# Copy of yn laid out by quarters, norm in place, rstd transfers ahead of reloads

## The chip, the cores and the metric

The kernel runs on one core of a Trainium2 chip. The time is device microseconds of one execution. Three runs of the kernel before gave 1457.63, 1461.26 and 1462.50 us; the median is 1461.26 us. The engines are named as in the profile: PE (TensorE), ACT (ScalarE), DVE (VectorE), POOL (GpSimd) and SP (SyncE, which here only issues DMAs; its queue is written SPq).

## The reference

One ConvNeXt V2 block on an image of 512 x 512 pixels with 96 channels, in bf16:

```
out = depthwise 3x3 convolution of x with dw          (96 channels)
h   = (out - mean) / sqrt(var + 1e-5)                 (over the 96 channels of a pixel)
h   = gelu(h @ w1)                                    (96 -> 384)
gx  = sqrt(sum of h*h over all pixels + 1e-6)         (one value for each of 384 channels)
nx  = gx / (mean of gx + 1e-6)
h   = (gamma * (h * nx) + beta + h) @ w2              (384 -> 96)
result = x + h
```

gx needs every pixel before the second matmul can begin, so there are two passes over the image.

## The kernel before, in words

**Units of work.** The image is cut into 128 blocks of four rows; two blocks, eight rows, make a pair d, of which there are 64. The first pass (about 0 to 880 us) goes in slots s: two slots to a pair, one block's matmul and gelu in each. The second pass (about 940 us to the end) takes the 128 blocks again, multiplies by w2 and writes the output.

**First pass, pair d.** SP loads x (`load_x`, four DMAs of 32 partitions into a tile `xin`). DVE turns it so that channels lie on partitions (`turn_x`), PE does the convolution (`conv_taps`), ACT and DVE evacuate it into a tile `y_bf` of [128, 2, 3, 512]. Partition 32q + p holds quarter q (two image rows and 16 channels); the second index, `ee`, is the even or odd channels; the third the group of 32 channels. For odd channels the quarters are turned round by two. POOL squares `y_bf` into `ysq` (`stage_sq`), PE sums both over channels (`stage_stats`), and for each two pairs (a batch k) DVE forms the variance, POOL the reciprocal root (`stage_rstd`, `stage_newton`), and DVE turns it (`stage_turn`).

**rstd and the normalised copy.** `stage_rows` writes the turned rstd to DRAM (`r_dram`, four DMAs for a batch), `stage_bcast` reads it back onto all partitions (`rbc`, four DMAs). `stage_norm` multiplies on POOL `y_bf` by `rbc` into a tile `yn`, once for even and once for odd channels. `stage_write` copies `yn` to DRAM (`yn_dram`): one DMA of 128 partitions for the even channels and two of 64 for the odd ones, whose halves are swapped. `stage_read` (`read_yn`) loads a block back as `ynT`, channels on 96 partitions, in two DMAs. The mean is not subtracted here; the weights `w1p` take it out. The channels of `ynT` come in the order of the planes, and w1 is loaded in that same order by six small DMAs. Six `ynT` tiles go round; 6 `y_bf`, 3 `yn`.

**MLP of the first pass.** `mlp_units` makes of a block six units: PE multiplies `ynT` by `w1p` into PSUM, ACT does the gelu of 128x1024 into `g`. DVE (`bst`) and PE (the gram matrix) gather the sums of squares. One block in three has its `g` stored to DRAM (`g_dram`, three DMAs, `store_next`).

**Order.** The order on each engine is that of the program. What goes into slot s is set by a table (`put`). For the batch of pairs d0 and d0+1 in the steady state: rows in slot 2*d0+7, broadcast in 2*d0+8, norms in 2*d0+9 and 2*d0+11, the writes in the slot after each norm, reloads of the even block one slot after the write and of the odd block two after, its MLP two slots after the reload. So in an odd slot SP issues: four loads of x, a store of `g`, the two reloads of an even block, and then, every second time, four rows. In an even slot: two reloads of an odd block, every second time four broadcasts, the write of the even channels, a store of `g`, the two writes of the odd channels. SP is one queue: an instruction that waits holds up all behind it. At most eight of its DMAs are under way, because they go round eight semaphores and each waits for the one eight places before it.

**Second pass.** Of the 128 blocks one in three has `g` loaded back (`gl`, POOL's queue), five are held, and the others load `ynT` again through `read_yn` (`load_rest`) and recompute `g` into `gr`. POOL adds the bias to x (`xb`), DVE adds it to the product (`o_sb`), SP writes the output.

Of the kernel before, what the change touches and what calls it, by code (L numbers as in the profile page):

```python
# [53 lines left out]
def kernel(  # L54
# [13 lines left out]
    bf16 = x.dtype  # L68
    assert bf16 == mybir.dt.bfloat16

    B, H, W, C = x.shape
# [3 lines left out]
    NI = C // 32  # L75
# [3 lines left out]
    ND = NBLK // 2  # L79
# [3 lines left out]
    QW = GR * 128  # L83
    NQ = GR * W // QW
    dram = ctx.enter_context(tc.tile_pool(name="dram", bufs=1, space=bass.MemoryType.DRAM))
    yn_dram = dram.tile([ND, 2 * NI, 4, 32 * W], bf16, name="yn_dram")
    r_dram = dram.tile([len(BATCHES), R8 * BATCH * W], bf16, name="r_dram")

    TAIL0 = NBLK - NTAIL
# [25 lines left out]
    def quad_out(flat_ap):  # L115
        return flat_ap.rearrange("p (g r m) -> p g r m", r=GR, m=MB)

    PLANE = 4 * 32 * W

    def read_yn(eng, t, q):  # L120
        base = yn_dram[q // 2]
        for h in range(2):
            eng.dma_start(out=t[:C, 2 * h:2 * h + 2, :].rearrange("c r w -> c (r w)"),
                          in_=bass.AP(base.tensor, base.offset + (2 * (q % 2) + h) * 32 * W,
                                      [[2 * W, 16], [PLANE, 2 * NI], [1, 2 * W]]))

    consts = ctx.enter_context(tc.tile_pool(name="consts", bufs=1))
    prepool = ctx.enter_context(tc.tile_pool(name="pre", bufs=1))
# [3 lines left out]
    w1_raw = consts.tile([C, E], bf16, name="w1_raw")  # L132
# [45 lines left out]
    with ExitStack() as p1:  # L178
        pe, dve, act, pool, sp = (InOrder(tc, e) for e in (nc.tensor, nc.vector, nc.scalar, nc.gpsimd, nc.sync))
# [22 lines left out]
        pc = p1.enter_context(ExitStack())  # L202
# [8 lines left out]
        def load_x(d):  # L211
            t = xinpool.tile([128, 2, SL, C], bf16, name="xin")
            off = lambda r, k, s: x.offset + ((R8 * d - 1 + 2 * r + k) * W - 1 + s) * C
            if d in (0, ND):
                k = 1 - d // ND
                if d == 0:
                    dve.memset(t[0:32, 0].rearrange("p g c -> p (g c)").bitcast(f32), 0.0)
                    pool.memset(t[0:1, 1, 0, :], 0.0)
                else:
                    pool.memset(t[0:32].rearrange("p k g c -> p (k g c)").bitcast(f32), 0.0)  # L220
                p0, s0, s1 = (16, 0, 1) if d == 0 else (0, SL - 1, SL)
                a, n = (1, SL - 1) if d == 0 else (0, SL - 1)
                sp.dma_start(out=t[0:32, k, a:a + n, :].rearrange("p g c -> p (g c)"),
                             in_=bass.AP(x.tensor, off(0, k, a), [[PXP * C, 32], [1, n * C]]))
                for p0, p1 in ((1, 16), (16, 32)) if d == 0 else ((0, 16), (16, 31)):
                    sp.dma_start(out=t[p0:p1, k, s0, :],
                                 in_=bass.AP(x.tensor, off(0, k, s0) + p0 * PXP * C, [[PXP * C, p1 - p0], [1, C]]))
            if d == 0:
                for r in range(1, 4):
                    load_pair(t, d, r, act if r > 1 else sp)  # L230
            elif d < ND:
                for r in range(4):
                    load_pair(t, d, r)
            xins[d] = t
# [18 lines left out]
        with nc.allow_low_precision("sums of zeros and a one"):  # L253
            dve.tensor_reduce(out=mask18, in_=ident_f[:18, :18].rearrange("p (k t) -> p k t", k=2), axis=AX.X, op=ALU.add)
            for q in range(4):
                dve.tensor_reduce(out=eye16[32 * q:32 * q + 32, :],
                                  in_=ident_f[32 * q:32 * q + 32, 32 * q:32 * q + 32].rearrange("p (c k) -> p c k", k=2),
# [8 lines left out]

        cen = consts.tile([C, 128], bf16, name="cen")
        xtpool = pc.enter_context(tc.tile_pool(name="xt", side="right", bufs=1))
        ypool = pc.enter_context(tc.tile_pool(name="ybf", side="right", bufs=6))
        ysqpool = pc.enter_context(tc.tile_pool(name="ysq", side="right", bufs=3))  # L270
        small = pc.enter_context(tc.tile_pool(name="small", side="right", bufs=2))
        rtpool = pc.enter_context(tc.tile_pool(name="rt", side="right", bufs=2))
        rbcpool = pc.enter_context(tc.tile_pool(name="rbc", side="right", bufs=3))
        ynpool = pc.enter_context(tc.tile_pool(name="yn", side="right", bufs=3))
        XT = [(0, 2), (2, 3), (5, 2)]
        xt_all = xtpool.tile([128, 7, SL * MB * 2], bf16, name="xT")
        assert 7 * SL * MB * 2 >= NQ * NCH * QW
# [20 lines left out]
        def load_rest(n, sq, pq):  # L298
            q = ORDER[n]
            v = grp.setdefault(q, {})  # L300
            if is_held(q):
                v["g"] = gs[q]
            elif is_whole(q):
                v["g"] = late.gl.tile([128, NQ, NCH, QW], bf16, name="gl")
                pq.dma_start(out=v["g"][:].rearrange("p t j w -> p (t j w)"), in_=g_dram[whole.index(q)])
            else:
                ynt = yn_ring[SLOTS[nth_made[q] % NYT]]
                if q not in KEPT:
                    read_yn(sq, ynt, q)
                v["ynt"] = ynt  # L310
# [92 lines left out]
        for i, (ee, G) in enumerate(UNITS):  # L403
            c0 = 32 * G + ee
            dve.tensor_tensor(out=dwx[:, i].rearrange("p (q c k) -> p q c k", q=4, k=2),
                              in0=dw18[:, None, c0:c0 + 31:2, None].to_broadcast([18, 4, 16, 2]),
                              in1=mask18[:, None, None, :].to_broadcast([18, 4, 16, 2]), op=ALU.mult)
            pe.matmul(Ud[:, i, :], lhsT=dwx[:, i], rhs=taps18, start=True, stop=True)
        for i in range(0, 2 * NI, NI):
            dve.tensor_tensor(out=Wq[:, i:i + NI].rearrange("p i d t (c o) -> p (i d t) c o", o=2),  # L410
                              in0=eye16[:, None, :, None].to_broadcast([128, 6 * NI, 16, 2]),
                              in1=Ud[:, i:i + NI].rearrange("p i (n o) -> p (i n) o", o=2)[:, :, None, :].to_broadcast(
                                  [128, 6 * NI, 16, 2]), op=ALU.mult)

        for ee in range(2):
            for G in range(NI):
                pool.dma_start(out=w1_raw[NI * ee + G:C:2 * NI, :], in_=w1[32 * G + ee:32 * G + 32:2, :])
        pool.dma_start(out=w2_sb[:], in_=w2.rearrange("(j p) c -> p j c", p=128))
        with nc.allow_non_contiguous_dma("tiny gamma/beta load"):
            pool.dma_start(out=gam_bf[:], in_=grn_gamma.rearrange("(j p) -> p j", p=128))  # L420
# [35 lines left out]
        ybf, ysq, yns, rbcs, msts, rns, rts = ({} for _ in range(7))  # L456
# [162 lines left out]
        def stage_rows(k):  # L619
            n = BATCHES[k][1]  # L620
            rt = rts.pop(k)
            with nc.allow_non_contiguous_dma("small rows of rstd"):
                for t in range(2 * n):
                    sp.dma_start(
                        out=r_dram[k, :2 * n * 32 * 128].rearrange("(t q a p) -> t a q p", q=32, a=4, p=32)[t],
                        in_=rt[:, 32 * t:32 * t + 32])

        def stage_bcast(k):
            n = BATCHES[k][1]
            rbc = rbcpool.tile([128, 2, BATCH // 2, W], bf16, name="rbc")  # L630
            base = r_dram[k]
            for q in range(4):
                sp.dma_start(out=rbc[32 * q:32 * q + 32].rearrange("p e d w -> p (e d w)"),
                             in_=bass.AP(base.tensor, base.offset + q * 4 * n * W,
                                         [[0, 16], [2 * n * W, 2], [1, 2 * n * W]]))
            rbcs[k] = rbc

        def stage_norm(d, eng=None):
            k = batch_of[d]
            i = d - BATCHES[k][0]  # L640
            y = ybf.pop(d)
            for ee in range(2):
                yn = ynpool.tile([128, NI, W], bf16, name="yn")
                (eng or pool).tensor_tensor(out=yn[:], in0=y[:, ee],
                                            in1=rbcs[k][:, ee, i:i + 1, :].to_broadcast([128, NI, W]), op=ALU.mult)
                yns[d, ee] = yn

        def stage_write(d, ee):
            yn = yns.pop((d, ee))
            base = yn_dram[d]  # L650
            step = 64 if ee else 128
            for p0 in range(0, 128, step):
                sp.dma_start(out=bass.AP(base.tensor, base.offset + ee * NI * PLANE + (p0 + 64 * ee) % 128 * W,
                                         [[W, step], [PLANE, NI], [1, W]]),
                             in_=yn[p0:p0 + step, :, :])

        def stage_read(b):
            t = yn_ring[b % NYT]
            read_yn(sp, t, b)
            ynts[b] = t  # L660
# [186 lines left out]
        with nc.allow_low_precision("sums of zeros and a one"):  # L847
            dve.tensor_reduce(out=rowsel[:, :R8].rearrange("p (q r) -> p q r", r=2),
                              in_=ident_f[:].rearrange("p (q c r) -> p q r c", q=4, r=2), axis=AX.X, op=ALU.add)
        dve.tensor_copy(out=rowsel[:, R8:], in_=rowsel[:, :GR])  # L850
        load_x(3)
        def next_x(s):
            if s % 2 and (s + 7) // 2 <= ND:
                load_x((s + 7) // 2)

        alone = 0
        for s in range(last_slot + 1):
            get = lambda kind: at.get((s, kind), [])
            early = s < FIRST_MLP + 6
            if not early:  # L860
                next_x(s)
            if early or s % 2 == 0:
                for b in get("read"):
                    stage_read(b)
            for k in get("bcast"):
                stage_bcast(k)
            for d in get("write"):
                stage_write(d, 0)
            store_next()
            for d in get("write"):  # L870
                stage_write(d, 1)
            if early:
                next_x(s)
            elif s % 2:
                for b in get("read"):
                    stage_read(b)
            for k in get("rows"):
                stage_rows(k)
            for k in get("newton"):
                stage_rstd(k, pool)  # L880
                stage_newton(k, pool)
# [2 lines left out]
            for d in get("norm"):  # L884
                stage_norm(d)
            mlp = get("mlp")

            def spread_out():
                for k in get("spread"):
                    stage_spread(k)  # L890
                for d in get("norma"):
                    stage_norm(d, dve)
# [114 lines left out]
        r = gi[:].bitcast(f32)  # L1007
        for it in range(3):
# [5 lines left out]
            r = rn_[:]  # L1014
# [75 lines left out]
```

## Time and profile before

| what | value |
| --- | --- |
| median of three runs | 1461.26 us |
| the profiled execution | 1462.48 us, span 1460.6 us |
| granted clock of the profiled execution | 0.986 |
| busy, whole span | PE 91%, ACT 91%, POOL 89%, DVE 74% |
| DMA moved | 430.82 MB, mean 295 GB/s |
| first pass, 300 to 500 us | ACT 192.09 of 200 us, POOL 191.88, PE 187.33, DMA share 0.93 |
| second pass, 940 to 1200 us | PE 245.22 of 260 us, POOL 242.14, ACT 238.40, DMA share 0.99 |
| `yn_dram<-yn` | 64 DMAs of 384 KB and 128 of 192 KB |
| `ynT<-yn_dram` | 420 DMAs of 192 KB: 268 in the first pass and around the turn, 152 in the second |
| `stage_norm` on POOL (`yn<-y_bf,rbc`) | 124 of 3104 ns |

Almost every instruction carries L36, the line of the helper that records the order, so groups are told apart by tile names. A row of the waits says which engine waited, for whom, how long in total, how many times and the longest. In the timeline of SP the second column is the time that the named DMAs took to issue, waits included; SP moves no data itself.

### The profile page before, as it was taken

The numbers are of one execution on the slowest core, as the hardware profiler recorded it, in microseconds if no ns is written. First come the engines' busy times: TensorE is split into PE (matmuls) and PEld (weight loads), VectorE is DVE, ScalarE is ACT, GpSimd is POOL, SyncE is SP. The second block draws the span as 40 slices with busy tenths as digits, with TensorE's granted clock in tenths as the row PEclk, the third lists the DMA queues.
The fourth block names the chain that finished last, engine by engine and source line by source line (L and its number), as shares of the span: only waits on it lengthen the run. The fifth ranks groups of instructions, "written<-read, shape, count | busy, mean of one in ns | idle before, by whom it ended". The sixth has DMA issues, their size and how long they took to land.

```text
span 1460.6 us, 55999 instructions
## 1 busy us (share of the span) xinstructions
PE 1334.5 (91%) x24212; PEld 871.7 (60%) x24212; DVE 1080.6 (74%) x2052; ACT 1333.3 (91%) x1235; POOL 1299.0 (89%) x899
## 2 busy tenths in 40 slices
PE   7879999999999999989999987889999989899998
PEld 3445555555555555555555554567777667666676
DVE  5768988988889898888889878745555545455455
ACT  4879999999999999999999999989999888888897
POOL 3499999999999999999999995489999999899997
PEclk8899999999999999999999999999999999999999
DMA  7779899998899998999899766499999999999997
GB/s 175 212 219 283 275 286 274 277 287 269 271 299 272 277 290 268 281 280 275 261 275 299 228 190 192 162 355 331 344 373 391 393 383 362 378 378 370 395 366 303
DMA packets 194103, 430.82 MB, mean 295 GB/s; under 512 B 39184, under 2 KB 88944, under 8 KB 188992
## 3 DMA queue, kind: packets, MB, share of 16 engines
q1 hardware_dynamic: 178044, 318.50, 69.6%
q0 software_dynamic: 15616, 108.29, 19.9%
q8 instruction: 190, 3.11, 0.9%
q10 hardware_dynamic: 196, 0.45, 0.1%
q14 instruction: 57, 0.47, 0.1%
HBM read 265.70 MB, written 161.45 MB: 292 GB/s over the span
## 4 chain that ended last, share of the span: by engine, by line
PE 42%; DMA 22%; ACT 18%; POOL 7%; DVE 4%; issue 3%; SPq 2%; ACTq 0%; DVEq 0%; POOLq 0%
PE PS L36 42%; ACT g L36 13%; DMA out_dram<-o_sb 11%; DMA ynT<-yn_dram 7%; ACT y_bf L36 4%; POOL xb L339 3%; DMA xin<-in_x_dram 3%; SPq L36 2%; POOL yn L36 2%; DVE bst L36 2%; DVE o_sb L36 1%; POOL ysq L36 1%; DMA rbc<-r_dram 1%; ACT xT L36 1%; ACT ysq L36 0%
## 5 line engine op out<-in xcount | busy, mean ns | idle before, releaser
L36 ACT ACTIVATE g<-PS 128x1024 bf16<-128x1024 f32 (+1 forms) x722 | 705.5, 1055 | 34.3 <-PE PS L36 20.2
L36 DVE BATCH_NORM_STATS2 bst<-g 128x6 f32<-128x512 bf16 x885 | 547.0, 677 | 46.8 <-ACT g L36 46.7
L36 PE MATMUL PS<-ynT,w1p 128*128 128x512 bf16 x1920 | 544.8, 381 | 39.0 <-ACT g L36 23.0
L36 ACT ACTIVATE gr<-PS 128x1536 bf16<-128x1536 f32 x348 | 485.8, 1450 | 47.6 <-PE PS L36 42.3
L36 DVE TENSOR_TENSOR o_sb<-PS,xb 128x384 bf16<-128x384 f32 x512 | 275.7, 557 | 244.8 <-PE PS L36 172.2
L36 POOL TENSOR_TENSOR yn<-y_bf,rbc 128x1536 bf16<-128x1536 bf16 x124 | 382.3, 3104 | 14.2 <-DMA rbc<-r_dram 13.2
L339 POOL TENSOR_TENSOR xb<-xr,B2c 128x1536 f32<-128x1536 bf16 x118 | 368.4, 3132 | 17.2 <-DVE o_sb L36 15.7
L36 POOL TENSOR_TENSOR ysq<-y_bf 128x1536 bf16<-128x1536 bf16 x120 | 327.1, 2747 | 38.1 <-DVE y_bf L36 38.1
L36 PEld LDWEIGHTS <-gr 128*128 128x128 bf16 x4152 | 206.6, 99 | 82.6 <-issue 31.5
L36 PE MATMUL PS<-xT,Wq 32*32 32x511 bf16 (+1 forms) x9216 | 235.9, 396 | 10.7 <-DVE xT L36 3.8
L36 PEld LDWEIGHTS <-w1p 128*128 128x128 bf16 x1920 | 148.4, 98 | 152.6 <-issue 89.2
L36 PE MATMUL PS<-W2s,gr 128*128 128x96 bf16 x4080 | 216.6, 207 | 23.6 <-DVE o_sb L36 23.3
L36 PE MATMUL PS<-w1p,ynT 128*128 128x384 bf16 (+2 forms) x1272 | 192.7, 273 | 27.6 <-ACT g L36 22.2
L36 PEld LDWEIGHTS <-Wq 32*32 32x32 bf16 x9216 | 100.2, 89 | 142.8 <-issue 64.8
L36 PEld LDWEIGHTS <-g 128*128 128x128 bf16 x2626 | 161.9, 98 | 34.2 <-issue 4.2
L36 PE MATMUL PS<-g 128*128 128x128 bf16 (+1 forms) x2386 | 173.2, 222 | 1.8 <-DVE warm L36 1.2
L36 PEld LDWEIGHTS <-ynT 128*128 128x128 bf16 x1272 | 102.0, 97 | 105.2 <-issue 82.6
L36 ACT ACTIVATE y_bf<-PS 128x1024 bf16<-128x1024 f32 (+1 forms) x141 | 137.4, 984 | 25.2 <-PE PS L36 25.2
L36 DVE STREAM_TRANSPOSE xT<-xin 128x576 f32<-128x576 f32 (+1 forms) x195 | 145.0, 771 | 6.2 <-DMA xin<-in_x_dram 4.9
L36 PEld LDWEIGHTS <-gl 128*128 128x128 bf16 x1824 | 89.4, 98 | 32.3 <-issue 9.4
L36 PE MATMUL PS<-W2s,gl 128*128 128x96 bf16 x1824 | 96.5, 206 | 7.7 <-DVE o_sb L36 7.5
L36 DVE CAST y_bf<-PS 128x512 bf16<-128x512 f32 x115 | 78.1, 679 | 5.8 <-PE PS L36 5.1
(108 smaller groups left out, 571.6 us busy)
## 6 DMA issues: line engine op xcount, KB each, us to landing
ynT<-yn_dram SPq DMA_DIRECT2D x420, 192.0 KB
g_dram<-g SPq DMA_DIRECT2D x114, 512.0 KB
gl<-g_dram POOLq DMA_DIRECT2D x38, 1536.0 KB, 11.3
xin<-in_x_dram SPq DMA_DIRECT2D x253, 216.0 KB
out_dram<-o_sb SPq DMA_DIRECT2D x127, 384.0 KB
xr<-in_x_dram POOLq DMA_DIRECT2D x123, 384.0 KB, 7.1
yn_dram<-yn SPq DMA_DIRECT2D x64, 384.0 KB
yn_dram<-yn SPq DMA_DIRECT2D x128, 192.0 KB
```

The costliest lines, as they stand in the source:

```text
L36: r = f(*a, **k)
L339: pq.tensor_tensor(out=xb[:], in0=grp[q]["xr"][:], in1=bias[:, None, :].to_broadcast([128, PXP, C]), op=ALU.add)
```

## The change

The DRAM copy of the normalised rows has its axes in the order quarter, plane instead of plane, quarter. A pair is written by four DMAs of 32 partitions, each of all six planes (192 KB), instead of one of 128 and two of 64 partitions. A block is read by one DMA for the even and one for the odd channels, each of 48 partitions (every second one) and two quarters, instead of one for each two rows on 96 partitions. The channels of `ynT` are then in their natural order, and w1 is loaded by one DMA. `stage_norm` writes its product over `y_bf`; the tile `yn` is gone, and `y_bf` has seven buffers instead of six. In the slot, broadcasts come before the reload of the odd block, and rows before the reload of the even block.

```diff
-    yn_dram = dram.tile([ND, 2 * NI, 4, 32 * W], bf16, name="yn_dram")
+    yn_dram = dram.tile([ND, 4, 2 * NI, 32 * W], bf16, name="yn_dram")
...
-    PLANE = 4 * 32 * W
+    PLANE = 32 * W
...
-        for h in range(2):
-            eng.dma_start(out=t[:C, 2 * h:2 * h + 2, :].rearrange("c r w -> c (r w)"),
-                          in_=bass.AP(base.tensor, base.offset + (2 * (q % 2) + h) * 32 * W,
-                                      [[2 * W, 16], [PLANE, 2 * NI], [1, 2 * W]]))
+        for ee in range(2):
+            quarter = 2 * ((q + ee) % 2)
+            eng.dma_start(out=t[ee:C:2, :, :].rearrange("c r w -> c (r w)"),
+                          in_=bass.AP(base.tensor, base.offset + (quarter * 2 * NI + ee * NI) * PLANE,
+                                      [[2 * W, NI * 16], [2 * NI * PLANE, 2], [1, 2 * W]]))
...
-        ypool = pc.enter_context(tc.tile_pool(name="ybf", side="right", bufs=6))
+        ypool = pc.enter_context(tc.tile_pool(name="ybf", side="right", bufs=7))
...
-        ynpool = pc.enter_context(tc.tile_pool(name="yn", side="right", bufs=3))
...
-        for ee in range(2):
-            for G in range(NI):
-                pool.dma_start(out=w1_raw[NI * ee + G:C:2 * NI, :], in_=w1[32 * G + ee:32 * G + 32:2, :])
+        pool.dma_start(out=w1_raw[:], in_=w1[:])
...
-                yn = ynpool.tile([128, NI, W], bf16, name="yn")
-                (eng or pool).tensor_tensor(out=yn[:], in0=y[:, ee],
+                (eng or pool).tensor_tensor(out=y[:, ee], in0=y[:, ee],
                                             in1=rbcs[k][:, ee, i:i + 1, :].to_broadcast([128, NI, W]), op=ALU.mult)
-                yns[d, ee] = yn
-
-        def stage_write(d, ee):
-            yn = yns.pop((d, ee))
+            yns[d] = y
+
+        def stage_write(d, h):
             base = yn_dram[d]
-            step = 64 if ee else 128
-            for p0 in range(0, 128, step):
-                sp.dma_start(out=bass.AP(base.tensor, base.offset + ee * NI * PLANE + (p0 + 64 * ee) % 128 * W,
-                                         [[W, step], [PLANE, NI], [1, W]]),
-                             in_=yn[p0:p0 + step, :, :])
+            for q in (h, h + 2):
+                sp.dma_start(out=bass.AP(base.tensor, base.offset + q * 2 * NI * PLANE,
+                                         [[W, 32], [PLANE, 2 * NI], [1, W]]),
+                             in_=yns[d][32 * q:32 * q + 32].rearrange("p e g w -> p (e g) w"))
+            if h:
+                yns.pop(d)
...
+            for k in get("bcast"):
+                stage_bcast(k)
             if early or s % 2 == 0:
                 for b in get("read"):
                     stage_read(b)
-            for k in get("bcast"):
-                stage_bcast(k)
...
-            elif s % 2:
+            for k in get("rows"):
+                stage_rows(k)
+            if not early and s % 2:
                 for b in get("read"):
                     stage_read(b)
-            for k in get("rows"):
-                stage_rows(k)
```

## The prediction

> **What bounds the kernel now.** I first read the stages. Between 165 and 822 us the first pass runs evenly; I cut it at 299.8 us because the pace changes there.
>
> ```profile
> core 0: us, PE busy (x) PEld busy (x) DVE busy (x) ACT busy (x) POOL busy (x), PEclk, DMA share, GB/s
> 165.40:299.80 134.40, 127.77 (x2664) 77.67 (x2664) 123.28 (x230) 131.12 (x141) 129.95 (x96) 1.00 0.92 277
> 299.80:822.50 522.70, 486.84 (x10105) 296.22 (x10104) 465.18 (x853) 498.41 (x533) 496.42 (x360) 1.00 0.91 277
> ```
>
> ACT is busy for 97.6% of the first stretch and 95.4% of the second. In the groups of ACT the two stretches hold 20 and 76 evacuations y_bf<-PS of 128x1024, one for each slot: 134.4 / 20 = 6.72 us a slot, then 522.7 / 76 = 6.88 us. So something takes 0.16 us a slot from 300 us on, 12 us in all, and every engine has room (ACT needs 498.41 / 76 = 6.56 us a slot, POOL 6.53, PE 6.41). The chain of waits says what it is:
>
> ```profile
> 485.36 5.31 DMA ynT<-yn_dram
> ...
> 512.53 5.23 DMA ynT<-yn_dram
> 517.76 0.14 issue
> 517.90 6.31 PE PS L36 x111
> ...
> 539.98 5.31 DMA ynT<-yn_dram
> ```
>
> Every 27.4 us, four slots, PE starts a block the moment its reload has landed. These are the even blocks of each second pair. I set the landing of each reload (the last signal of its semaphore before that semaphore is used again) against the first gelu of its block, which comes at least 0.81 us later: for those blocks the gap falls from 3.3 us at 162 us to 0.8 at 326 us and then stays mostly there. The three other blocks of four have medians of 3.7, 7.8 and 6.5 us. Why is the reload late? SP's timeline over one period, 504.50 to 531.90 us:
>
> ```profile
> 504.50 0.58 SPq L36 DMA_DIRECT2D yn_dram<-yn  x1
> 505.12 0.48 SPq L36 DMA_DIRECT2D g_dram<-g  x1
> 505.71 1.87 SPq L36 DMA_DIRECT2D yn_dram<-yn  x2
> 507.68 3.60 SPq L36 DMA_DIRECT2D xin<-in_x_dram  x4
> 511.38 0.37 SPq L36 DMA_DIRECT2D g_dram<-g  x1
> 511.89 2.81 SPq L36 DMA_DIRECT2D ynT<-yn_dram  x4
> ...
> 518.05 2.65 SPq L36 DMA_DIRECT2D xin<-in_x_dram  x4
> 520.80 0.37 SPq L36 DMA_DIRECT2D g_dram<-g  x1
> 522.63 2.41 SPq L36 DMA_DIRECT2D ynT<-yn_dram  x2
> 525.09 2.30 SPq L36 DMA_DIRECT2D r_dram<-rt  x4
> 527.49 1.79 SPq L36 DMA_DIRECT2D ynT<-yn_dram  x2
> 529.38 2.48 SPq L36 DMA_DIRECT2D rbc<-r_dram  x4
> ```
>
> 34 DMAs in 27.4 us, and SP hardly rests: one opening of 1.46 us before 522.63. SP issues the writes of 504.50 about 2 us after POOL has finished that pair, so it lags the engines rather than waiting for them. **SP's queue sets the pace of the steady state**, with the DMA engines (share 0.91) close behind. Two waits that the change touches:
>
> ```profile
> POOL yn L36 <- DMA rbc<-r_dram: 13.2, 11, 4.0
> PE PS L36 <- DMA ynT<-yn_dram: 10.6, 13, 2.1
> ...
> SPq L36 <- DMA yn_dram<-yn: 61.7, 52, 3.7
> ```
>
> **The change part by part.** Costs are for one period of four slots (two pairs), 19 of which lie between 299.8 and 822.5 us.
>
> *Four writes for three.* Two more DMAs on SP a period. Issuing one takes 0.61 us (median over the 192 writes of before) and about 0.06 us passes to the next: 1.34 us. Below: nothing, if the time above the median (1.87 and 2.01 us for the second two writes, 0.65 and 0.79 above 2 x 0.61) is SP held back by busy DMA engines, so that an issue more only shortens that. Above: 2 x 1.0, at the rate of those rows. I take 1.34, since most issue rows in the period lie near their shortest. Queued behind it are the x loads and, after these, the critical reload.
>
> *Their packets.* 768 packets of 1 KB for a pair, as before. In the trace's packet records the packets of the 128-partition write last 47 ns in the mean, those of the two 64-partition writes 55. All at 55 adds 4 ns x 1536 / 16 engines = 0.4 us of DMA time a period. Upper end: the 32-partition x loads, whose 3456-byte packets last 216 ns in the mean against 135 for their quickest; by that ratio, 1.6 x 46 = 74 ns, 2.2 us a period. Lower end: 47 ns, -0.4 us. I take 55 ns, the row of the same direction and packet, and 0.3 us on the path, because DMA has 9% free.
> [...]
>
> *Rows ahead of the even reload.* The reload at 522.63 came after the opening of 1.46 us, 0.92 us of it a wait for a write to land. Four rows, 2.30 us, now go into that opening: -0.92 us. Bounds: -1.46, and 0 if the broadcast now waits for its rows instead. Two reloads still stand between the last row and the first broadcast, as before. The even reload behind the rows comes 2.30 - 0.92 = 1.4 us later; it feeds a block with 3.7 - 0.8 = 2.9 us to spare, so PE does not notice; if that were used up, PE would pay up to 1.4 us a period.
>
> *Broadcast ahead of the odd reload.* That reload comes 2.5 us later, with 7.8 - 0.8 = 7.0 us to spare: nothing. rbc comes about 4 us earlier, which ends POOL's waits of 13.2 us; 9.2 of them lie in the steady state, where POOL has 26 us free and another queue sets the pace: nothing there. One of 4.0 us lies in the tail (around 863 us), on the chain: -2 us, between 0 and -4.
>
> *Norm in place.* POOL's product stays 128x1536. Nearest rows: 2748 ns (ysq, both inputs one buffer) and 3132 ns (xb); now 3104. At worst 28 ns x 120 = 3 us of POOL time, hidden by its 26 us. The tile is freed after its write has landed instead of after the norm, with one buffer more; the pair seven on evacuates into it four slots after the write slot for the first pair of a batch: nothing. The first write now waits for both halves; SP came 2 us after both.
>
> *Reloads by channel parity.* Still two DMAs of 96 packets of 2 KB onto the same 96 partitions. Nothing for the first pass. In the second pass DMA is busy at 0.99, and 15168 such packets last 99.5 ns in the mean, the quickest 84. If the new walk moved every packet to 84 or as far the other way, that is 15.5 ns x 948 = 15 us either way; both walks put the same six partitions on an engine, if these are dealt out in order, so I take 0.
>
> *One load of w1 for six.* POOL then waits 38.1 us for y_bf in any case: nothing. *Ramp:* two writes more, while ACT and PE carry the chain: nothing, at most 1.2 us.
>
> **Sum.** A period: 1.34 + 0.3 - 0.92 = +0.7 us; 19 x 0.7 = 13.7 us. From 165 to 300 us SP already loses about 0.5 us a period (3.3 to 0.9 us of spare in five periods); with 0.7 more the spare is gone after two, and the other three run at 27.5 + 0.7 against 26.9: +4 us. Tail -2. Together +15.7 on the profiled execution's 1462.5 (its span of 1460.6 and 1.9 around it), which is 1.2 above the median: 1478, and 1477 as a median. I say 1476.
>
> **The rivals.**
> 1. [...] 2.2 instead of 0.3 us a period: 19 x (1.34 + 2.2 - 0.92) = 50 us if all of it shows, of which DMA's 9% (2.5 us a period) hides perhaps half: 1485 to 1505, say 1492. For it: DMA at 0.91 and all four writes on 32 partitions. Against: the writes alternate between lower and upper half of the partitions, as the two 64-partition writes do at 55 ns.
> 2. *The other side: the queue gets shorter.* If SP's slow issues (xin 3.60 against 2.65 us for the same four) are back pressure, the two issues more cost nothing, and the opening filled by the rows takes the 0.92 us off. It decides when a period falls below 4 x 6.72 = 26.9 us, that is by 0.6 us; then ACT sets the pace again: -12 us, the tail -2: 1448. For it: 52 waits for a write to land, 61.7 us. Against: the critical reload has no such opening before it (511.38, then 511.89), but two issues more.
> 3. *Nothing:* the gain of 0.92 and the issues of 1.34 cancel within the stalls. 1459 to 1465.
>
> [...]
>
> **How the numbers follow.** Forecast (slower by 5 to 25 us) 0.43, rival 1 0.19, rival 2 0.25, no difference 0.13. A change of 0.3% (4.4 us) is what this kernel's measurement can tell from none. Slower 0.43 + 0.19 = 0.62, same 0.13, faster 0.25. The range goes from rival 2 at 1448 to 1497, inside rival 1; about a tenth lies beyond each end. The forecast's own range is 1466 to 1486.
>
> **What would show it.** In the profile after: slots between 300 and 822 us of 7.05 us (rival 2: 6.72); the wait of PE for ynT well above 10.6 us; the wait of POOL for rbc under 5; SP's wait for yn_dram under 40 us; issue of the four writes near 2.6 us; 1 KB packets near 55 ns (rival 1: 70 or more). Wrong I would be if SP's slow issues vanish with the new writes, or if the second pass, which I leave at 521 us, moves by more than 5.

## The result and the profile after

The changed kernel takes 1499.63 us (median of four runs, 1497.38 to 1507.88) against 1461.88 us for the kernel before in the same comparison (1457.63 to 1464.02): 1.0278 of it, interval 1.0246 to 1.031. The forecast of 1476 us had the direction right and the size less than half; the time lies above the range given, and inside rival 1 (1485 to 1505).

The profiled execution after is the slowest of the four: 1507.88 us, span 1506.1, granted clock 0.973. Its stages, cut as those of before (20 and 76 evacuations `y_bf<-PS` of 128x1024):

```profile
core 0: us, PE busy (x) PEld busy (x) DVE busy (x) ACT busy (x) POOL busy (x), PEclk, DMA share, GB/s
172.40:317.40 145.00, 130.89 (x2665) 78.52 (x2664) 124.52 (x227) 131.28 (x140) 131.44 (x96) 0.97 0.88 264
317.40:856.60 539.20, 494.42 (x10105) 297.73 (x10103) 464.91 (x852) 498.98 (x532) 494.19 (x362) 0.98 0.90 267
```

145.0 / 20 = 7.25 us a slot (before 6.72) and 539.2 / 76 = 7.09 (before 6.88). The work did not grow: ACT is busy for 498.98 us as before for 498.41, POOL for 494.19 against 496.42. Every engine idles more, and DMA moves less (267 against 277 GB/s) at nearly the same share (0.90 against 0.91). The first stretch, where before still ran at ACT's pace, lost more per slot than the second. The first pass (to the first `o_sb`) ends at 969.7 instead of 937.6 us: 32 us. The second pass takes 533.0 instead of 519.3 us, but in the eleven profiles shown or told of here whose second pass is that of before, its length lies between 515 and 534 us, so a difference of 14 between two single ones says little.

SP's queue in the steady state, one period of four slots, 499.87 to 528.53 us (28.66 us, before 27.4; columns: start, time to issue with waits, what, how many):

```profile
499.87 2.10 SPq L36 DMA_DIRECT2D yn_dram<-y_bf  x2
...
502.55 2.06 SPq L36 DMA_DIRECT2D yn_dram<-y_bf  x2
504.70 3.11 SPq L36 DMA_DIRECT2D xin<-in_x_dram  x4
...
511.48 1.02 SPq L36 DMA_DIRECT2D yn_dram<-y_bf  x2
512.59 0.51 SPq L36 DMA_DIRECT2D g_dram<-g  x1
513.15 2.21 SPq L36 DMA_DIRECT2D yn_dram<-y_bf  x2
...
518.08 0.37 SPq L36 DMA_DIRECT2D g_dram<-g  x1
518.96 2.72 SPq L36 DMA_DIRECT2D r_dram<-rt  x4
522.30 1.96 SPq L36 DMA_DIRECT2D ynT<-yn_dram  x2
524.38 2.77 SPq L36 DMA_DIRECT2D rbc<-r_dram  x4
527.20 1.22 SPq L36 DMA_DIRECT2D ynT<-yn_dram  x2
528.53 1.02 SPq L36 DMA_DIRECT2D yn_dram<-y_bf  x2
```

Eight writes take 2.10 + 2.06 + 1.02 + 2.21 = 7.39 us; six took 0.58 + 1.87 + 0.53 + 2.01 = 4.99. That is 2.4 us a period, not 1.34. The pairs at 1.02 us are at their shortest; those near 2.1 were held up, by what these lines do not say. The opening ahead of 518.96 is 0.51 us where it was 1.46, so the rows did move into it, and the period is 1.3 us longer all the same. The waits (engine, releaser, total us, times, longest):

```profile
PE PS L36 <- DMA ynT<-yn_dram: 32.6, 19, 3.5
...
PEld L36 <- DMA ynT<-yn_dram: 27.4, 14, 3.6
POOL y_bf L36 <- DMA rbc<-r_dram: 27.1, 19, 3.3
...
SPq L36 <- DMA yn_dram<-y_bf: 17.7, 11, 3.8
```

PE waits 32.6 us for reloads (before 10.6). The 27.4 us of its weight loads (before 3.7) do not add to that: 26.0 of them fall in the same moments. SP waits less for writes to land (before 61.7), so it is not that wait that holds the queue back. POOL's wait for `rbc`, which was to go, doubled (before 13.2).

### The profile page after: what moved, and what is told of

It reads as the page before. It is cut to its first block, busy times and chain, and to the rows that moved or that the text cites. A ratio compares the mean times of both kernels' runs of the same rounds, so it can differ in the third digit from the quotient of the medians.

```text
span 1506.1 us, 56055 instructions
## 1 busy us (share of the span) xinstructions
PE 1351.3 (90%) x24212; PEld 876.4 (58%) x24212; DVE 1082.8 (72%) x2052; ACT 1334.7 (89%) x1235; POOL 1295.6 (86%) x894
## 4 chain that ended last, share of the span: by engine, by line
PE 42%; DMA 28%; ACT 17%; SPq 4%; DVE 4%; issue 3%; POOL 2%; ACTq 0%; DVEq 0%; POOLq 0%
PE PS L36 42%; DMA out_dram<-o_sb 14%; ACT g L36 11%; DMA ynT<-yn_dram 9%; ACT y_bf L36 4%; SPq L36 4%; DVE o_sb L36 1%; DMA r_dram<-rt 1%; DVE bst L36 1%; DMA g_dram<-g 1%; ACT gr L36 1%; DMA xin<-in_x_dram 1%; POOL ysq L36 1%; ACT xT L36 1%; POOL y_bf L36 1%
## 5 line engine op out<-in xcount | busy, mean ns | idle before, releaser
L36 PE MATMUL PS<-ynT,w1p 128*128 128x512 bf16 x1920 | 549.2, 384 | 60.6 <-DMA ynT<-yn_dram 32.6
L36 POOL TENSOR_TENSOR y_bf<-y_bf,rbc 128x1536 bf16<-128x1536 bf16 x124 | 381.9, 3101 | 27.1 <-DMA rbc<-r_dram 27.1
L36 PE MATMUL PS<-xT,Wq 32*32 32x511 bf16 (+1 forms) x9216 | 242.0, 406 | 9.7 <-DVE xT L36 4.8
L36 PE MATMUL PS<-w1p,ynT 128*128 128x384 bf16 (+2 forms) x1272 | 196.1, 276 | 26.8 <-ACT g L36 21.4
```

The costliest lines, as they stand in the source:

```text
L36: r = f(*a, **k)
```

## The experiments

Each ratio is to the kernel before on the same chip. The experiments ran on three chips, so a comparison of two ratios takes it that the ratio does not depend on the chip. "First pass" is the start of the first `o_sb` in the profile of each kernel. The "gap" of a block is, as in the prediction, the time from the landing of its reload to its first gelu; 0.8 us is no room at all.

The first expectations name three theories. Q: the two issues more a period on SP and the slower small writes carry the loss. O: the new order makes a second reload of four critical and so carries it. P: the norm in place carries it.

### The parts, one at a time

**Norm in place alone.** Before, with

```diff
-                yn = ynpool.tile([128, NI, W], bf16, name="yn")
-                (eng or pool).tensor_tensor(out=yn[:], in0=y[:, ee],
+                (eng or pool).tensor_tensor(out=y[:, ee], in0=y[:, ee],
...
-                yns[d, ee] = yn
+                yns[d, ee] = y[:, ee]
```

and seven `y_bf` buffers, no `yn`.

> The kernel before with the norm written over y_bf (seven y_bf buffers, no yn tiles), three writes, old order. Theories Q and O: 1459 to 1465 us, POOL's product still 3.10 us. Theory P: 1475 to 1495 us, POOL, ACT or DVE waiting for yn_dram writes.

Measured: 1456.96 against 1457.21 us, 0.9994 (0.9973 to 1.0015). It costs nothing, as the prediction has it. Its one profile shows more: the gap of the critical block rises from 0.8 to 3.1 us (medians), PE waits 0.3 us for reloads, and the first pass ends at 929.1 us, 8.5 earlier than in the profile of before. The median time shows none of it. Whether single first passes scatter by as much, or the gain is lost elsewhere, is not settled; a difference of less than 10 us between two first passes shows nothing by itself.

**The new order alone.** Before, with broadcasts ahead of the odd reload and rows ahead of the even one:

```diff
+            for k in get("bcast"):
+                stage_bcast(k)
             if early or s % 2 == 0:
...
-            for k in get("bcast"):
-                stage_bcast(k)
...
-            elif s % 2:
-                for b in get("read"):
-                    stage_read(b)
             for k in get("rows"):
                 stage_rows(k)
+            if not early and s % 2:
+                for b in get("read"):
+                    stage_read(b)
```

> The kernel before with the new order alone: three writes, yn tiles and reloads as before. Theory Q: 1452 to 1463 us, no loss, SP's wait for yn_dram under 40 us (61.7 before). Theory O: 1478 to 1495 us, PE's wait for ynT over 25 us (10.6 before), the even reload behind the rows now without room. Theory P: 1462.

Measured: 1468.38 against 1457.21 us, 1.0074 (1.0045 to 1.0103): slower, where the prediction counted a gain, and between the ranges of theories Q and O. SP's wait for writes fell from 61.7 to 37.9 us and POOL's for `rbc` from 13.2 to 7.7, as they were meant to; PE's for reloads rose from 10.6 to 15.0. The gap of the even block whose reload now stands behind the rows falls from 3.6 to 2.1 us (medians) and is under 1.2 us in 4 of 24 blocks, before in none: a second reload of four is now late at times, as theory O has it, though far from always. The odd block's gap falls from 7.6 to 4.7. In its one profile the first pass ends 3 us later than before (940.5), so where the 11 us lie is not settled by it.

**Four writes alone.** Before, with the even channels also written in two halves of 64 partitions:

```diff
-            step = 64 if ee else 128
+            step = 64
```

> The kernel before with the even channels written in two DMAs of 64 partitions instead of one of 128: four writes for a pair, nothing else. Theory Q: 1480 to 1492 us (two issues more a period, 1.34 to 2.4 us x 19 periods, and the early loss). Theory O: 1462 to 1468. Theory P: 1462 to 1465.

Measured: 1487.36 us, 1.0205 (1.0177 to 1.0234). This one line makes most of the loss: 30 us. Its first pass ends at 959.7 us.

**All but the order.** The changed kernel with rows and broadcasts back behind the reloads (the lines of the second diff undone).

> The changed kernel with one part undone: rows and broadcasts stand behind the reloads again, as before. Theory Q (the two more DMA issues a period on SP and the slower 32-partition writes carry the loss): 1490 to 1500 us, as the changed kernel; slots between 317 and 857 us of about 7.1 us. Theory O (the new order makes a second reload of four critical and so carries the loss): 1465 to 1480 us, and PE's wait for ynT back near 10 us. Theory P (norm in place carries it): as the changed kernel, 1495 to 1500.

Measured: 1484.08 us, 1.0185 (1.0159 to 1.0212), first pass 958.5 us. The time lies between the ranges of Q and O, and it agrees with the four writes alone (1.0205). So the layout by quarters, the reload by channel parity, 32 partitions in place of 64, the norm in place and the single load of w1 together cost nothing that can be told from zero. What is left to the order in the changed kernel is 1.0278 against 1.0185, with intervals that do not touch; its first pass ends 11 us later with the order than without (969.7 against 958.5). The gap of the even block behind the rows falls here from 3.7 to 2.0 us and is under 1.2 us in 4 of 23 blocks, without the order in none.

### The order

**Rows ahead, broadcasts where they were.** Of the order's diff only the lines of `rows` and the even reload.

> The kernel before with the rows alone moved ahead of the even reload; broadcasts stay behind the odd reload. Together the two moves cost 11 us. If the rows carry it (the even reload behind them comes later, its room falls from 3.7 to near 2 us, two reloads of four become critical): 1463 to 1470 us. If the broadcasts carry it (SP stands before the odd reload until the rows have landed): 1455 to 1460, and room of the even reload as before.

Measured: 1462.32 against 1461.42 us, 1.0007 (0.9981 to 1.0033): nothing. SP's wait for writes falls to 33.8 us, and no time comes of it.

**Broadcasts ahead, rows where they were.** Only the lines of `bcast`.

> The kernel before with the broadcasts alone moved ahead of the odd reload; now no reload stands between the last row and the first broadcast. If the broadcasts carry the 11 us: 1463 to 1475 us (SP waits about 2 us a period for the rows to land, 19 x 2 = 38 us of queue at the most). If the rows carry it: 1455 to 1460.

Measured: 1487.18 us, 1.0186 (1.0137 to 1.0236), worse than either expectation. Its SP queue says why. The rows now stand right ahead of the broadcast that reads them back:

```profile
513.56 2.45 SPq L36 DMA_DIRECT2D r_dram<-rt  x4
516.50 2.86 SPq L36 DMA_DIRECT2D rbc<-r_dram  x4
519.41 1.23 SPq L36 DMA_DIRECT2D ynT<-yn_dram  x2
```

and SP waits for them to land:

```profile
SPq L36 <- DMA r_dram<-rt: 42.9, 27, 2.7
```

A wait that did not exist before now holds up everything behind it on the queue. With the rows ahead too, two reloads stand between and that wait is gone (0.4 us with the order alone, 0.6 after). So the two moves are not two gains: the one that matters is harmful alone, and the other one takes more than half of the harm back.

**Norm in place and rows ahead, together**, the two parts that cost nothing.

> The kernel before with the two parts of the change that cost nothing alone: norm in place (0.9994) and rows ahead of the even reload (1.0007). Both theories: 1452 to 1463 us, no difference; if their small reliefs of SP add up where SP sets the pace, up to 8 us faster.

Measured: 1465.85 against 1458.79 us, 1.0039 (1.0009 to 1.007). That is a little above the range expected. They do not add up to a gain; none of the kernels here is faster than the one before by more than the noise.

### The fourth write: the issue, or the data?

**One issue more.** Before, with one small DMA a pair on SP:

```diff
+            if ee == 0:
+                sp.dma_start(out=extra_dram[d], in_=yn[0:32, 0, 0:32])
```

It copies 2 KB that nothing reads.

> The kernel before with one more DMA on SP for each pair, behind the write of the even channels, that copies 2 KB of yn to a place nobody reads: 32 packets of 64 bytes, so hardly any DMA time (32 x 11 ns / 16). The output is unaffected. If an issue on SP alone costs what the fourth write costs: 1480 to 1492 us (+20 to +30) and slots of 7.0 us or more between 300 and 822 us. If the 64- and 32-partition packets or DMA time carry it: 1460 to 1466.

Measured: 1468.3 against 1458.79 us, 1.0072 (1.004 to 1.0105). That is between the two expectations: an issue more a pair costs about 10 us, a third of the fourth write's 30. Its first pass ends at 934.2 us, not later than before's.

**One issue less in the changed kernel.** One of the four x loads goes to POOL's queue:

```diff
-                    load_pair(t, d, r)
+                    load_pair(t, d, r, pool if r == 3 else sp)
```

> The changed kernel with one of the four x loads of each pair issued by POOL instead of SP: SP has as many issues a period as in the kernel before, the bytes and their packets stay. POOL pays about 0.5 us for each (its issue of xr takes that), 0.25 us a slot on 6.53, and has room at 7.1. If SP's issues carry the fourth write's cost: 1470 to 1482 us, slots near 6.85. If packets or DMA time carry it: 1494 to 1505.

Measured: 1486.31 us, 1.0198 (1.014 to 1.0255), against 1.0278 for the changed kernel: 0.8% back, with intervals that just touch, and between the two expectations. The first pass still ends late, at 960.9 us. With as many issues on SP as before, some 70% of the loss stays.

**Fewer, larger stores of g.** Two of 768 KB instead of three of 512, which takes one issue off SP for every block that is stored; on the kernel before and on the changed one:

```diff
-                n = NCH * QW * NQ // 3
+                n = NCH * QW * NQ // 2
...
-                    stores.extend((b, h) for h in range(3))
+                    stores.extend((b, h) for h in range(2))
```

> The kernel before with g stored in two DMAs of 768 KB instead of three of 512 KB: same bytes, 1.33 issues fewer a period on SP. If the number of issues on SP sets the pace: first pass at 6.7 us a slot all through and 1445 to 1456 us. If bytes or DMA time set it: 1456 to 1462, or slower through the longer bursts.

> The changed kernel with g stored in two DMAs instead of three: same bytes, 1.33 issues fewer a period, which takes back two thirds of the two issues that the change adds. If the number of issues on SP carries the cost of the fourth write (27 to 30 us): 16 to 22 us faster than the changed kernel, 1477 to 1485. If DMA time or the 32-partition writes carry it: 1494 to 1502, as the changed kernel.

Measured: 1470.49 us, 1.0069 (1.0041 to 1.0097) on before, and 1488.29, 1.0212 (1.0151 to 1.0274) on the changed one. On before fewer issues made it slower, by 0.7%: here what the queue carries weighs at least as much as how many DMAs it issues. On the changed kernel the time lies between the two expectations, and its interval overlaps with that of the change itself. These two also make each store larger (768 KB for 512), so they do not separate the causes cleanly; the next two do.

**The fourth write on all partitions.** Two cuts of the even write that leave issues, bytes and packets as in the run with four writes alone. By planes, two and one, 128 partitions each:

```diff
+                for g0, g1 in ((0, NI),) if ee else ((0, 2), (2, NI)):
+                    sp.dma_start(out=bass.AP(base.tensor, base.offset + (ee * NI + g0) * PLANE + (p0 + 64 * ee) % 128 * W,
+                                              [[W, step], [PLANE, g1 - g0], [1, W]]),
+                                  in_=yn[p0:p0 + step, g0:g1, :])
```

> The kernel before, with the write of the even channels cut in two by planes: one DMA of 128 partitions x 2 planes (256 KB) and one of 128 partitions x 1 plane (128 KB). Four writes a pair, the same 768 packets of 1 KB, every write but the two old ones of 64 on all 128 partitions. Where four writes a pair were made by cutting the even write into halves of 64 partitions, the time was 1.0205 of before and the packets lasted 56.7 ns in the mean; one small DMA more a pair cost 1.0072. Theory A (the half-partition transfers cost the rest): packets stay at 49 to 52 ns, the first pass ends at 933 to 945 us as in the run with the small DMA, ratio 1.004 to 1.010 (1464 to 1475 us). Theory B (any further write of real data costs the rest, whichever partitions it is on): first pass ends at 956 to 965 us, ratio 1.017 to 1.024 (1483 to 1496 us).

Measured: 1467.65 against 1457.68 us, 1.0071 (1.0035 to 1.0107). And by alternate partitions, 64 each:

```diff
+            if ee == 0:
+                for o in range(2):
+                    sp.dma_start(out=bass.AP(base.tensor, base.offset + o * W, [[2 * W, 64], [PLANE, NI], [1, W]]),
+                                  in_=yn[o:128:2, :, :])
+                return
```

> The kernel before, with the write of the even channels cut in two by alternate partitions: one DMA of partitions 0, 2, 4 ..., one of 1, 3, 5 ... (192 KB each). Size, count and issue are those of the halves 0 to 63 and 64 to 127, which gave 1.0205; only the partitions are spread over the whole range. Theory A (what costs is that a write covers only one half of the partitions): packets 49 to 53 ns, first pass 933 to 945 us, ratio 1.004 to 1.010. Theory B (the number of writes and their size costs, not the place): packets as may be, first pass 956 to 965 us, ratio 1.017 to 1.024. [...]

Measured: 1472.43 us, 1.0103 (1.0074 to 1.0132). Both are clear of 1.0205 (the second lies a little above the range of theory A), the first equals the run with the small DMA, and their first passes end at 941.3 and 942.0 us instead of 959.7. Here two writes of 64 partitions are cheap if the 64 are every second one (1.0103), and dear if they are one half (1.0205). **The place on the partitions makes the difference**: 1.0205 against 1.0103 and 1.0071, 1.0 to 1.3%, 15 to 19 us. Which rows of DRAM one DMA writes changes with the cut too; that this matters is not excluded by a run.

It can be seen in single writes. The windows below hold the first write of a pair, at a moment when its 384 packets stand apart from other writes; the last two numbers are the DMA share and GB/s. Before, one DMA of 128 partitions:

```profile
258.68:259.87 1.19, 1.00 (x17) 0.49 (x15) 1.19 (x3) 1.19 (x3) 1.19 (x1) 1.00 1.08 385
```

Four writes alone, halves 0 to 63 and 64 to 127:

```profile
266.29:268.38 2.09, 1.90 (x43) 0.84 (x42) 2.09 (x4) 2.09 (x3) 1.24 (x1) 1.00 0.94 245
```

By planes:

```profile
314.53:315.88 1.35, 1.35 (x50) 0.50 (x38) 1.20 (x2) 1.15 (x3) 1.35 (x1) 1.00 0.98 348
```

By alternate partitions:

```profile
263.10:264.53 1.43, 1.43 (x43) 0.73 (x41) 1.43 (x3) 1.43 (x2) 0.98 (x2) 1.00 1.01 337
```

The same bytes take 2.09 us in halves and 1.19 to 1.43 otherwise, and the DMA engines count as busy all the while (0.94 to 1.08). Taken as such first writes are all bursts of exactly 384 packets of 1 KB between 165 and 850 us that begin more than 5 us after the burst ahead began; a burst ends where no further such packet starts for 0.3 us. There are 17 to 22 in each of the four kernels, and the medians are 1.36 us before, 2.37 in halves, 1.47 by planes, 1.45 by alternate partitions, with packets of 46.2, 69.8, 46.7 and 47.5 ns; in the changed kernel, with 32 partitions each, 2.54 us and 65.2 ns (8 of them). So a lone first write in halves takes 1.74 times as long as on 128 partitions (2.37 against 1.36 us) and 1.63 times as long as by alternate partitions (1.45 us). What in the hardware makes the half slow, the traces do not show.

And it arrives where the time is lost. Waits for the reload, in halves:

```profile
PE PS L36 <- DMA ynT<-yn_dram: 27.4, 18, 3.0
...
PEld L36 <- DMA ynT<-yn_dram: 20.5, 14, 3.0
```

and by planes:

```profile
PE PS L36 <- DMA ynT<-yn_dram: 13.0, 11, 2.0
...
PEld L36 <- DMA ynT<-yn_dram: 6.1, 6, 2.0
```

By alternate partitions PE waits 15.3 us. As above, most of a PEld row lies in the same moments as the PE row.

## Why the prediction was wrong

**What bounds the kernel: right in part.** With the halves and with the order, PE waits longer for `ynT` (27.4 and 15.0 us, before 10.6). But the wait is not the whole price: with the norm in place alone it is nearly gone (0.3 us) and the time stays, and with one issue more PE waits less than before (7.6 against 10.6 us) while the time grows by 10. Nor did parts that relieve SP's queue (rows ahead, fewer stores) bring time.

**"Their packets", 0.3 us a period: the step whose mechanism failed.** It set the price by the mean of all packets (47 ns on 128 partitions, 55 on 64) and took a quarter off because DMA has 9% free: 6 us over 19 periods. Measured: 15 to 19 us, spread over the 24 periods of the steady state 0.6 to 0.8 us each. The means themselves hold: over all 1 KB packets between 200 and 820 us, 51.6 ns before and 56.7 with four writes. But they hide what a write that stands alone shows, 69.8 ns against 46.2. By those bursts a pair would cost 1.0 us more, 48 us over 24 periods, so more than half of that is hidden after all. How the rest reaches the reload stays open: the time that SP takes to issue a write between 200 and 820 us is almost the same in halves (0.78 us) as by alternate partitions (0.75). The 6 us that the prediction took were about a third of the price. Rival 1 looked for the loss in the right place, longer packets of the writes, and took their length from the x loads (74 ns; those of a lone write were 65.2 to 69.8); that the x loads are slow for their 32 partitions, no run shows. That the time lies in its range is partly luck: it counts 25 us for the issues, where 10 to 15 were measured, and a gain of some 17 us for the rows, which did not come.

**"Four writes for three", 1.34 us a period: too large.** It made 25 us of 19 periods; one issue more on SP measures 10 us (1.0072, and 1.0071 by planes), two full-spread writes for one by alternate partitions 15. The eight writes after take 2.4 us a period more, but that holds the slow transfers as well as the issues.

**"Rows ahead", -0.92 us a period: the term furthest off.** The sum made a gain of some 17 us of it. The opening was filled, SP's wait for writes fell as foretold (17.7, under 40), and rows alone gave 1.0007. The likely reason, argued and not tested, is that the reload behind the opening had 2.9 us to spare by the prediction's own count, so that the opening was no time on the path. And that room was less safe than "PE does not notice" has it: in the changed kernel it is used up in 4 of 23 blocks.

**"Broadcast ahead", 0 and -2: wrong sign.** The whole order costs 0.7% on before and 0.9% on the changed kernel, 11 to 14 us, where the sum had it save some 19. The broadcast stands where it pushes the odd reload and, with the rows behind the reload, waits itself. POOL's wait for `rbc` doubled in the changed kernel, but not by the order: with the four writes alone it is 34.1 us, with the order alone 7.7.

**"Norm in place", "one load of w1": right**, 0.9994, and nothing between 1.0185 and 1.0205. **"Reloads by channel parity", 0: right**, as far as the second pass lets it be seen (521.5 us with it in the run without the order, 519.3 without). That partitions are dealt out to the DMA engines in order was an assumption; no trace shows it.

**What would show it.** Slots: 7.05 us forecast, 7.09 found (and 7.25 in the first stretch, where the 4 us forecast for 20 slots make 6.92). PE's wait for `ynT`: up, as said. SP's wait for writes under 40: as said, without profit. Issue of four writes: 3.7 us a pair, not 2.6. Packets of 1 KB: 55.5 ns in the mean between 200 and 820 us, as forecast, and yet the wrong thing to look at. POOL's wait for `rbc` under 5: 27.1. The second pass moved by 14 us, where more than 5 was named as a sign of being wrong; single second passes scatter by as much, so it decides nothing.

**The sum.** 30 (the fourth write: 10 to 15 for the write, the rest for the halves) + 11 to 14 (order) = 41 to 44 us, against 1461 x 0.0278 = 41 us measured (38 by the medians). The terms are differences between comparisons, each uncertain by 4 to 7 us, so their agreement is better than it has a right to be. Left open: where the smaller terms (the issue, the order alone) act. Their single profiles show a first pass within 4 us of before's and a second pass 10 to 14 us longer, in which the code is the same; the second pass of single executions scatters by as much.

## What to carry to other kernels

Here a write of 192 KB from one half of the partitions was not the same as one of the same size spread over all: for one of 384 KB, two by halves made the time 1.0205 of before's, two by alternate partitions 1.0103, and a cut by planes 1.0071. Where such a write has to be cut, try the free axis or alternate partitions before halves. The mean of packets priced it too low (6 us), the burst that stands alone too high (48), and only the same write cut in another way gave the price (15 to 19). A DMA share below one (0.91 here) did not tell how much of a slower transfer would be hidden, and filling an opening on the busy queue brought nothing by itself (1.0007). Look at what stands between the write and the read of a DRAM round trip on one queue: with nothing between them SP waited 42.9 us for the rows to land and the time was 1.0186, with two reloads between them 0.4 us and 1.0074.

## What the runs showed of the hardware that was not expected

In the changed kernel the granted clock fell from 1.00 to 0.50 after PE had waited 1.64 us for a reload:

```profile
401.51 1.01 PE L36 MATMUL PS<-ynT,w1p 128*128 128x512 bf16 x3 [1.64 <-DMA ynT<-yn_dram]
```

and the two stretches on either side of 402.0 us (the clock is the third number from the right):

```profile
398.60:402.00 3.40, 1.76 (x34) 1.22 (x32) 3.40 (x7) 1.85 (x3) 3.40 (x2) 1.00 1.07 306
402.00:405.40 3.40, 3.40 (x56) 1.22 (x66) 1.77 (x3) 1.97 (x3) 3.40 (x2) 0.50 1.07 382
```

In this trace's clock record a half-speed stretch of the steady state lasts 3.41 us, or twice that; with the two long ones taken as two each there are nine, and their starts lie whole multiples of 3.41 us apart (200.6, 204.0, 316.7, 402.0, 460.0, 572.7, 658.0, 661.4, 746.7). With the time cut into pieces along these starts, the seven that follow full speed come after a piece in which PE was busy for 0 to 1.77 us; no piece with 1.88 us or more led to one, and two with 1.57 and 1.67 did not either. (By alternate partitions, a piece with 1.95 us did lead to one, so in these traces the line lies between 1.5 and 2 us and is not sharp.) Between 110 and 860 us the clock is halved for 30.7 us in the changed kernel, 23.9 with the four writes alone, 6.8 by planes, 10.2 by alternate partitions and 3.4 before. So here a late reload was paid twice: as the wait, and by at most half of the stretch after it (up to 14 us of the change's 41; how much of that is on the path was not separated). PE's longer wait, 22 us, and this together are near the 32 us by which the first pass grew.
